# Squared-ReLU attention with a routed FFN: the last 64 keys move from the thirteenth to the eighth slot of a chunk

## The chip, the core and the metric

The kernel runs on one core of a Trainium2 chip. The metric is the time of one execution on the device in microseconds (us). Before the change it is 2067.73 us, the median of three runs (2067.33 to 2068.75). The five engines have queues of their own: PE multiplies matrices (its weight loads are listed as PEld), DVE, ACT and POOL work element by element, and SP issues the transfers.

## The reference, cut to what matters

```python
def _attn_ref(u, v, z):                      # u, v: 8 x 3136 x 256, z: 8 x 3136 x 64
    scale = 1.0 / S
    scores = scale * np.matmul(z, z.transpose(0, 2, 1))
    attn = np.maximum(scores, 0.0) ** 2
    return u * np.matmul(attn, v)

def _moe_ref(x, w_gate, w1, w2, capacity):   # capacity 128, F = 1024
    scores = np.einsum('bsd,d->bs', x, w_gate)
    out = x.copy()
    for b in range(B):
        top_idx = np.argpartition(-scores[b], capacity)[:capacity]
        xe = x[b, top_idx]
        ye = np.maximum(xe @ w1, 0.0) @ w2
        g = 1.0 / (1.0 + np.exp(-scores[b, top_idx]))
        out[b, top_idx] = x[b, top_idx] + g[:, None] * ye
    return out
```

For each of 8 batches, all 3136 keys weigh all 3136 queries by the square of a rectified product; the weighted sum of v is multiplied by u. Then the 128 tokens of the batch with the highest gate score go through a small FFN. All is float32.

## The kernel before

**Chunks and slots.** A batch is cut by queries into seven chunks: five of 512 columns (0 to 4), one of 256 and one of 320. For each chunk the 3136 keys are gone through in 13 *slots*: twelve with a pair of key tiles of 128 each, and one with the last 64 keys, which the code marks by `js == (NJ,)`. So there are 8 x 7 x 13 = 728 slots, in one list, `slots` (from line 319). Before the change the slot of 64 keys is the thirteenth of each chunk.

**What a slot does on PE.** float32 values are split into a high part `hi` and a low part `lo`, and v likewise. `mix` (line 523) adds a pair's share to the chunk's two accumulators, one for each half of the 256 columns of v: eight matmuls with `hi` and four with `lo`, all on line 556. The slot of 64 keys has four matmuls and no `lo` tile; its low half lies in the same tile as its high half. Its matmuls are also the last of the chunk: they carry `stop`, and `finish` (line 596) follows. In the first slot of a chunk (but the very first) the list is sorted by half, so a `lo` is read after four matmuls and not after eight. Three accumulator buffers serve all chunks: the second half of a new chunk needs the buffer that the first half of the old one frees.

**What it needs from the others.** A pair is *new* when its scores have to be made, or *old* when an earlier chunk has already made them (the score matrix is symmetric), stored them transposed, and they are fetched again. For a new pair, PE makes the scores with four matmuls (line 440) three slots ahead, in the middle of `mix`; ACT rectifies (line 450) and squares into `hi` (line 451); DVE squares once more in float32 (line 462), or ACT does (line 456); DVE or POOL subtracts to get `lo` (line 518); DVE transposes what later chunks want (lines 483 and 503), and SP stores it. For an old pair, ACT casts `hi` (line 418) and DVE or POOL makes `lo`. For the 64 keys, DVE does a square, a subtraction (line 474) and a transpose. An element-wise step goes to whichever of two engines a running tally, `busy`, says is less loaded.

**What sets the order.** The program is written out by hand, slot by slot, in the loop at the end (from line 1444). In slot k it issues first what `plan` holds for k: loads and preparations at fixed slot numbers, such as the next batch's z (`prep_z`, in the eighth slot of chunks 1 to 5, which puts a subtraction called ZL on POOL) and the chunk's u (`load_u`, in the eighth slot). Then comes `mix`, then the posts: the squares, `lo` parts and transposes of the pair three slots ahead, and with them DVE's share of a *near* task (multiplying a finished chunk by u, transposing it, the gate's sum) or a *far* task (choosing the tokens of the batch before, and its FFN). Far tasks run only in pair slots, and `rested` keeps them apart. Where the slot behind k is that of the 64 keys, the loop issues only the squares and holds the other posts back until that slot is over (lines 1502 to 1505):

```python
if k + 2 < len(slots) and len(slots[k + 1][2]) == 1:
    now = square_scores if c < WHOLE and (b or c) else settle_scores
    posts, held_posts = [now], [fn for fn in posts if fn is not settle_scores]
```

`finish` puts two instructions on DVE (line 601) that multiply the accumulators by u, and so free their buffers.

Of the kernel before, what the change touches and what calls it, by code (L numbers as in the profile page):

```python
# [88 lines left out]
def attention_then_routed_ffn(ctx: ExitStack, tc: tile.TileContext, zt, ut, v, wg, w1, w2, cst, cst16, keys, outs, at, cap):  # L89
    nc = tc.nc  # L90
    B, S, D = v.shape
# [14 lines left out]
    ROUNDS = 32 // BITS  # L106
    SHARES = P >> BITS
    SLOTS = NJ // 2 + 1

    const = ctx.enter_context(tc.tile_pool(name="const", bufs=1))  # L110
    vpool = ctx.enter_context(tc.tile_pool(name="vpool", bufs=NJ // 2))
# [204 lines left out]

    slots = []
    for b in range(B):  # L320
        for c in range(NCH):
            known = min(c, WHOLE) * GT + (2 if c > WHOLE and b < B - 1 else 0)
            old = [(2 * g, 2 * g + 1) for g in range(known // 2)]
            new = [(2 * g, 2 * g + 1) for g in range(known // 2, NJ // 2)]
            if c == WHOLE and b < B - 1:
                new.reverse()
            if c < WHOLE and (b or c):

                new.insert(len(new) - 2, new.pop(1))
            wait = 0.5 if (b, c) == (0, 1) else 0.0  # L330
            both = [(wait + (1 - wait) * (i + 0.5) / len(old), 0, js, True) for i, js in enumerate(old)]
            place = [(i + 0.5) / len(new) for i in range(len(new))]
            if b < B - 1 and c == NCH - 1:
                place = [1.6 / len(old)]
            both += [(x, 1, js, False) for x, js in zip(place, new)]
            slots += [(b, c, js, is_old) for _, _, js, is_old in sorted(both)]
            slots.append((b, c, (NJ,), False))
    assert len(slots) == B * NCH * SLOTS

    squares = [  # L340
# [185 lines left out]
    def mix(k, beside, between):  # L526


        b, c, js, _ = slots[k]
        assert k in parts  # L530
        hi, lo = parts.pop(k)
        first, last = k % SLOTS == 0, js[0] == NJ
        if first:
            acc[b, c] = [ps_a.tile([P, CH], F32, name="acc", tag="acc")[:, : CHUNKS[c][1]] for _ in range(NK)]
        ac = acc[b, c]
        todo = []
        if last:
            for h in range(NK):
                for w in range(2):
                    todo.append((h, V[b, NJ][:, w, h], hi[:, 0], w == 1))  # L540
        else:
            for h in range(NK):
                for q, j in enumerate(js):
                    for w in range(2):
                        todo.append((h, V[b, j][:, w, h], hi[:, q], False))
            for q, j in enumerate(js):
                for h in range(NK):
                    todo.append((h, V[b, j][:, 0, h], lo[:, q], False))
            if first and (b or c):
                todo.sort(key=lambda x: x[0])  # L550
        turn = (6 if c else 4) if first else 4 if last or len(slots[min(k + 1, len(slots) - 1)][2]) == 1 else 8
        done, lead, started = 0, 2, set()
        for n, (h, w, mov, stop) in enumerate(todo):
            if n == turn:
                between()
            nc.tensor.matmul(ac[h], w, mov, start=first and h not in started, stop=stop)  # L556
            started.add(h)
            upto = len(beside) * max(0, n - lead + 1) // (len(todo) - lead)
            for op in beside[done:upto]:
                op()  # L560
            done = max(done, upto)
        if turn == len(todo):
            if last:
                near.extend(finish(b, c))
            between()

    gate = {}
# [821 lines left out]
    def settle_stores():  # L1389
        for store in stores:  # L1390
            store()
        stores.clear()

    def took_by(k):
        _, c, js, is_old = slots[k]
        return CHUNKS[c][1] * 0.00045 * (6 if len(js) == 1 else 12 if is_old else 16)
# [53 lines left out]
    for k, (b, c, js, is_old) in enumerate(slots):  # L1450
# [8 lines left out]
        if len(js) == 2:  # L1459
            if near and (k % SLOTS or c <= NCH - late if late else k % SLOTS % 3 == 2):  # L1460
                tasks.append(near.popleft())
            if far and far[0] is None and not near and not tasks and not (late and c >= NCH - late):
                far.popleft()
                rested = k + 2
            if late and c >= NCH - late:

                left = sum(took_by(i) for i in range(k, k - k % SLOTS + SLOTS))
# [13 lines left out]
            elif (  # L1481
                far and far[0] and rested <= k and (busy["dve"] < 9 if late else not tasks)
                and (len(far[0]) < 4 or k % SLOTS != SLOTS - 3)
            ):
                task = far.popleft()
                rested = k + (task[2] if len(task) > 2 else 1 if late else 2)
                tasks.append(task[:2])
                if late and not near and rested == k + 1 and len(tasks) == 1 and far and not far[0][0] and busy["dve"] < 9:
                    tasks.append(far.popleft()[:2])
# [9 lines left out]
        now = settle_scores  # L1499
        posts = [*posts[:half], now, *posts[half:]]  # L1500
        held_posts = []
        if k + 2 < len(slots) and len(slots[k + 1][2]) == 1:

            now = square_scores if c < WHOLE and (b or c) else settle_scores
            posts, held_posts = [now], [fn for fn in posts if fn is not settle_scores]
# [9 lines left out]
        clock += took  # L1515
        if tasks:
            ready = max(told + 0.5, clock + 2.0)
        if len(js) == 1 and cap > 0:
            if c == NCH - 1 - late:
                far.extend([None, *route(b)])  # L1520
            elif c >= NCH - late:
# [64 lines left out]
```

## Time and profile before

| what | us |
|---|---|
| median of three runs | 2067.73 |
| the profiled execution | 2067.41 |
| its span | 2065.6 |
| PE busy in it | 2055.2 |
| DVE, POOL, ACT busy | 1529.0, 1357.5, 1291.2 |

The profiled execution lies 0.32 us under the median; 1.8 us of it lie around the span. A busy time is the union of an engine's instructions. Ends of matmuls are modelled, so two that follow each other closely overlap in the records, and a short wait may not show as idle time. Lines are those of the kernel before; in the changed kernel the same statements stand 1 to 6 lines lower in the part that matters here (556 becomes 562, 462 becomes 468, 601 becomes 607).

### The profile page before, as it was taken

The page shows a single profiled execution, that of the slowest core. Times are in us where ns is not written, and L with a number is a line of the kernel's source. Part 1 is how long each engine was busy: PE and PEld are TensorE (multiplying, and loading weights), DVE is VectorE, ACT ScalarE, POOL GpSimd, SP SyncE. Part 2 cuts the span into 40 slices and gives each one's busy share as a digit, 9 for nine tenths or more (in the row PEclk, how much of TensorE's full clock was granted, in tenths as well). Part 3 has the DMA queues.
Part 4 walks back from the last instruction along what each step waited for, and adds up shares of the span by engine and source line. Part 5 has one row for each costly group of instructions (what it writes and reads, how often), then busy time and mean ns, then how long its engine had stood idle before and what let it go on. Part 6 is the DMA issues. An engine that isn't in the chain of part 4 may idle for free.

```text
span 2065.6 us, 31660 instructions
## 1 busy us (share of the span) xinstructions
PE 2055.2 (99%) x10280; PEld 1744.5 (84%) x10280; DVE 1529.0 (74%) x2667; ACT 1291.2 (63%) x1629; POOL 1357.5 (66%) x728
## 2 busy tenths in 40 slices
PE   9999999999999999999999999999999999999999
PEld 6888988889888898888988889888898888888788
DVE  7676678856788667875678756887578876787776
ACT  7665576656775467664676546765477654775543
POOL 6766587756876468764677647875578755765643
PEclk9999999999999999999999999999999999999999
DMA  6788767886668765787767877678776776666862
GB/s 197 207 232 226 217 188 207 233 231 190 193 188 232 212 205 177 199 233 210 208 185 193 235 203 217 184 192 236 194 222 188 192 201 178 206 192 164 213 173 95
DMA packets 442758, 415.52 MB, mean 201 GB/s; under 512 B 133792, under 2 KB 374880, under 8 KB 439520
## 3 DMA queue, kind: packets, MB, share of 16 engines
q1 hardware_dynamic: 441456, 411.01, 70.9%
q0 software_dynamic: 768, 2.10, 0.3%
q8 instruction: 80, 1.31, 0.3%
q14 instruction: 86, 0.70, 0.1%
q10 hardware_dynamic: 368, 0.39, 0.1%
HBM read 238.78 MB, written 174.60 MB: 200 GB/s over the span
## 4 chain that ended last, share of the span: by engine, by line
PE 87%; DVE 3%; issue 2%; ACT 2%; DMA 2%; POOL 1%; SPq 1%; POOLq 0%; DVEq 0%; ACTq 0%
PE acc L556 73%; PE sc L440 12%; ACT hi L451 1%; POOL lo L518 1%; ACT a L450 1%; DVE a L462 1%; DVE aT L483 1%; PE h L1215 1%; PE y L1259 1%; DMA vst<-in_v 0%; DMA squares<-aT 0%; DVE lo L518 0%; DMA qk<-in_zt 0%; PE spread L680 0%; DMA qk<-squares_narrow 0%
## 5 line engine op out<-in xcount | busy, mean ns | idle before, releaser
L556 PE MATMUL acc<-hi,V 128*128 128x512 f32 (+2 forms) x5376 | 1218.4, 364 | 0.5
L518 POOL TENSOR_TENSOR lo<-a,hi 128x1024 fp32r<-128x1024 f32 (+2 forms) x326 | 717.9, 2204 | 563.5 <-DVE a L462 426.7
L556 PEld LDWEIGHTS acc<-hi,V 128*128 128x128 f32 x5376 | 932.9, 188 | 157.4 <-DVE ut L601 5.5
L556 PE MATMUL acc<-lo,V 128*128 128x512 f32 (+2 forms) x2688 | 664.0, 363 | 1.0 <-POOL lo L518 1.0
L450 ACT ACTIVATE a<-sc 128x1024 f32<-128x1024 f32 (+4 forms) x401 | 358.2, 893 | 449.2 <-PE sc L440 421.0
L556 PEld LDWEIGHTS acc<-lo,V 128*128 128x128 f32 x2688 | 471.1, 188 | 76.7 <-POOL lo L518 4.4
L462 DVE TENSOR_TENSOR a<-sc,a 128x1024 f32<-128x1024 f32 (+5 forms) x306 | 307.4, 1005 | 249.8 <-ACT hi L451 225.8
L418 ACT CAST hi<-qk 128x1024 fp32r<-128x1024 f32 (+2 forms) x327 | 279.7, 860 | 220.1 <-PE acc L556 198.1
L483 DVE STREAM_TRANSPOSE aT<-a 128x512 f32<-128x512 f32 (+3 forms) x541 | 349.5, 681 | 76.7 <-ACT a L456 54.4
L451 ACT ACTIVATE hi<-a 128x1024 fp32r<-128x1024 f32 (+4 forms) x401 | 372.2, 928 | 24.8 <-PE acc L556 2.3
L518 DVE TENSOR_TENSOR lo<-qk,hi 128x1024 fp32r<-128x1024 f32 (+2 forms) x220 | 319.2, 1459 | 81.7 <-ACT hi L418 79.3
L440 PE MATMUL sc<-Z,ZH 128*128 128x512 f32 (+2 forms) x746 | 275.1, 373 | 2.3 <-DVE a L462 2.1
L440 PE MATMUL sc<-Z,ZL 128*128 128x512 f32 (+2 forms) x746 | 273.3, 370 | 0.1
L518 POOL TENSOR_TENSOR lo<-qk,hi 128x1024 fp32r<-128x1024 f32 (+2 forms) x107 | 210.0, 1965 | 51.3 <-ACT hi L418 41.6
L440 PEld LDWEIGHTS sc<-Z,ZH 128*128 128x128 f32 x746 | 140.5, 188 | 31.7 <-DVE a L462 6.0
L440 PEld LDWEIGHTS sc<-Z,ZL 128*128 128x128 f32 x746 | 140.5, 188 | 24.7 <-DVE ZL L126 0.5
L126 POOL TENSOR_TENSOR V<-vst,V 128x512 fp32r<-128x512 f32 x92 | 136.5, 1489 | 29.8 <-ACT V L125 26.4
L622 POOL TENSOR_TENSOR ut<-x,w_run 128x1024 f32<-128x1024 f32 (+2 forms) x52 | 126.0, 2422 | 24.4 <-DVE x L613 23.4
L456 ACT ACTIVATE a<-a 128x1024 f32<-128x1024 f32 x93 | 98.8, 1062 | 2.9
L126 POOL TENSOR_TENSOR ZL<-zst,ZH 128x512 fp32r<-128x512 f32 (+2 forms) x56 | 84.2, 1508 | 2.5 <-ACT ZH L125 2.2
L125 ACT CAST V<-vst 128x512 fp32r<-128x512 f32 x95 | 57.9, 609 | 35.5 <-DMA vst<-in_v 35.5
L601 DVE SCALAR_TENSOR_TENSOR ut<-acc,ut 128x512 f32<-128x512 f32 (+2 forms) x112 | 63.9, 611 | 19.5 <-PE acc L556 19.2
(187 smaller groups left out, 1083.1 us busy)
## 6 DMA issues: line engine op xcount, KB each, us to landing
squares<-aT SPq DMA_DIRECT2D x160, 512.0 KB
qk<-squares SPq DMA_DIRECT2D x320, 256.0 KB
squares_narrow<-aT SPq DMA_DIRECT2D x320, 128.0 KB
qk<-squares_narrow SPq DMA_DIRECT2D x80, 512.0 KB
out<-x SPq DMA_DIRECT2D x162, 128.0 KB
ut<-in_ut SPq DMA_DIRECT2D x40, 512.0 KB
vst<-in_v SPq DMA_DIRECT2D x158, 128.0 KB
squares_own<-aT SPq DMA_DIRECT2D x39, 256.0 KB
```

The lines of the kernel that those rows point to most:

```text
L126: (lo_on or nc.vector.tensor_tensor)(lo, src, hi.bitcast(F32), op=ALU.subtract)
L418: nc.scalar.copy(by(hi), src)
L440: nc.tensor.matmul(ps[:, q], z[:, j * P : (j + 1) * P], mov, start=z is ZH, stop=z is ZL)
L450: nc.scalar.activation(a, ps[:, :n], AF.Relu)
L451: nc.scalar.activation(pieces[0][0](hi), pieces[0][1], AF.Square)
L456: nc.scalar.activation(a, a, AF.Square)
L462: square = lambda: nc.vector.tensor_tensor(a[rows], of[rows, :n], a[rows], op=ALU.mult)
L483: nc.vector.transpose(to, a[rows, q].rearrange("p (m t a) -> p m t a", m=GT, a=Q))
L518: on.tensor_tensor(view(lo), src, view(hi).bitcast(F32), op=ALU.subtract)
L556: nc.tensor.matmul(ac[h], w, mov, start=first and h not in started, stop=stop)
L601: nc.vector.scalar_tensor_tensor(xT[:, h, :w], acc[b, c][h], SCALE * SCALE, xT[:, h, :w], op0=ALU.mult, op1=ALU.mult)
L622: nc.gpsimd.tensor_tensor(wx, runs, consts["wg_run"].rearrange("p (o r) -> p o r", o=1).broadcast_to([P, NB, RUN]), op=ALU.mult,)
```

## The change

In chunks 1 to 4 of batches 0 to 6, the slot of 64 keys is put at index 7 of the chunk's 13 (`MIDDLE`), the eighth, and the pairs behind it move back by one. The chunk's last slot is then a pair: its last `lo` matmuls carry `stop`, its list is sorted by half like a first slot's, and `finish` follows it. The hold on posts ahead of the 64 keys does not apply in these chunks. `later` counts rests without the moved slot. All other chunks keep the old place.

```diff
--- before.py
+++ after.py
@@ -106,6 +106,7 @@
     ROUNDS = 32 // BITS
     SHARES = P >> BITS
     SLOTS = NJ // 2 + 1
+    MIDDLE = SLOTS // 2 + 1
 
     const = ctx.enter_context(tc.tile_pool(name="const", bufs=1))
     vpool = ctx.enter_context(tc.tile_pool(name="vpool", bufs=NJ // 2))
@@ -316,6 +317,10 @@
 
 
 
+    def inside(b, c):
+
+        return b < B - 1 and 0 < c < WHOLE
+
     slots = []
     for b in range(B):
         for c in range(NCH):
@@ -333,8 +338,9 @@
             if b < B - 1 and c == NCH - 1:
                 place = [1.6 / len(old)]
             both += [(x, 1, js, False) for x, js in zip(place, new)]
-            slots += [(b, c, js, is_old) for _, _, js, is_old in sorted(both)]
-            slots.append((b, c, (NJ,), False))
+            mine = [(b, c, js, is_old) for _, _, js, is_old in sorted(both)]
+            mine.insert(MIDDLE if inside(b, c) else len(mine), (b, c, (NJ,), False))
+            slots += mine
     assert len(slots) == B * NCH * SLOTS
 
     squares = [
@@ -529,15 +535,15 @@
         b, c, js, _ = slots[k]
         assert k in parts
         hi, lo = parts.pop(k)
-        first, last = k % SLOTS == 0, js[0] == NJ
+        first, last, rest = k % SLOTS == 0, k % SLOTS == SLOTS - 1, js[0] == NJ
         if first:
             acc[b, c] = [ps_a.tile([P, CH], F32, name="acc", tag="acc")[:, : CHUNKS[c][1]] for _ in range(NK)]
         ac = acc[b, c]
         todo = []
-        if last:
+        if rest:
             for h in range(NK):
                 for w in range(2):
-                    todo.append((h, V[b, NJ][:, w, h], hi[:, 0], w == 1))
+                    todo.append((h, V[b, NJ][:, w, h], hi[:, 0], last and w == 1))
         else:
             for h in range(NK):
                 for q, j in enumerate(js):
@@ -545,10 +551,10 @@
                         todo.append((h, V[b, j][:, w, h], hi[:, q], False))
             for q, j in enumerate(js):
                 for h in range(NK):
-                    todo.append((h, V[b, j][:, 0, h], lo[:, q], False))
-            if first and (b or c):
+                    todo.append((h, V[b, j][:, 0, h], lo[:, q], last and q == 1))
+            if first and (b or c) or last:
                 todo.sort(key=lambda x: x[0])
-        turn = (6 if c else 4) if first else 4 if last or len(slots[min(k + 1, len(slots) - 1)][2]) == 1 else 8
+        turn = (6 if c else 4) if first else 4 if rest or len(slots[min(k + 1, len(slots) - 1)][2]) == 1 else 8
         done, lead, started = 0, 2, set()
         for n, (h, w, mov, stop) in enumerate(todo):
             if n == turn:
@@ -559,9 +565,9 @@
             for op in beside[done:upto]:
                 op()
             done = max(done, upto)
+        if last:
+            near.extend(finish(b, c))
         if turn == len(todo):
-            if last:
-                near.extend(finish(b, c))
             between()
 
     gate = {}
@@ -1391,6 +1397,13 @@
             store()
         stores.clear()
 
+    def later(k, n):
+
+        while n:
+            k += 1
+            n -= not (k < len(slots) and len(slots[k][2]) == 1 and inside(*slots[k][:2]))
+        return k
+
     def took_by(k):
         _, c, js, is_old = slots[k]
         return CHUNKS[c][1] * 0.00045 * (6 if len(js) == 1 else 12 if is_old else 16)
@@ -1461,7 +1474,7 @@
                 tasks.append(near.popleft())
             if far and far[0] is None and not near and not tasks and not (late and c >= NCH - late):
                 far.popleft()
-                rested = k + 2
+                rested = later(k, 2)
             if late and c >= NCH - late:
 
                 left = sum(took_by(i) for i in range(k, k - k % SLOTS + SLOTS))
@@ -1483,7 +1496,7 @@
                 and (len(far[0]) < 4 or k % SLOTS != SLOTS - 3)
             ):
                 task = far.popleft()
-                rested = k + (task[2] if len(task) > 2 else 1 if late else 2)
+                rested = later(k, task[2] if len(task) > 2 else 1 if late else 2)
                 tasks.append(task[:2])
                 if late and not near and rested == k + 1 and len(tasks) == 1 and far and not far[0][0] and busy["dve"] < 9:
                     tasks.append(far.popleft()[:2])
@@ -1499,7 +1512,7 @@
         now = settle_scores
         posts = [*posts[:half], now, *posts[half:]]
         held_posts = []
-        if k + 2 < len(slots) and len(slots[k + 1][2]) == 1:
+        if k + 2 < len(slots) and len(slots[k + 1][2]) == 1 and not inside(b, c):
 
             now = square_scores if c < WHOLE and (b or c) else settle_scores
             posts, held_posts = [now], [fn for fn in posts if fn is not settle_scores]
@@ -1515,7 +1528,7 @@
         clock += took
         if tasks:
             ready = max(told + 0.5, clock + 2.0)
-        if len(js) == 1 and cap > 0:
+        if k % SLOTS == SLOTS - 1 and cap > 0:
             if c == NCH - 1 - late:
                 far.extend([None, *route(b)])
             elif c >= NCH - late:
```

How this moves instructions, at three places of batch 2. First PE, at the end of chunk 1 and the start of chunk 2 (`Vr` is the part of v of the 64 keys, `acc` the accumulators, `sc` scores of a later slot). Before:

```order
L556 MATMUL acc_5693<-lo_6035,V_5476 128x512
L556 MATMUL acc_5694<-lo_6035,V_5476 128x512
L556 MATMUL acc_5693<-hi_6049,Vr_5542 128x512 x2
L556 MATMUL acc_5694<-hi_6049,Vr_5542 128x512 x2
L440 MATMUL sc_6122<-Z_5910,ZH_96 128x512
L440 MATMUL sc_6122<-Z_5910,ZL_97 128x512
L440 MATMUL sc_6122<-Z_5910,ZH_96 128x512
L440 MATMUL sc_6122<-Z_5910,ZL_97 128x512
L556 MATMUL acc_6156<-hi_6085,V_5138 128x512 x4
L556 MATMUL acc_6156<-lo_6098,V_5138 128x512 x2
```

Now:

```order
L562 MATMUL acc_5693<-hi_6029,V_5476 128x512 x4
L562 MATMUL acc_5693<-lo_6052,V_5476 128x512 x2
L562 MATMUL acc_5694<-hi_6029,V_5476 128x512 x2
L446 MATMUL sc_6117<-Z_5918,ZH_96 128x512
L446 MATMUL sc_6117<-Z_5918,ZL_97 128x512
L446 MATMUL sc_6117<-Z_5918,ZH_96 128x512
L446 MATMUL sc_6117<-Z_5918,ZL_97 128x512
L562 MATMUL acc_5694<-hi_6029,V_5476 128x512 x2
L562 MATMUL acc_5694<-lo_6052,V_5476 128x512 x2
L562 MATMUL acc_6151<-hi_6068,V_5138 128x512 x4
L562 MATMUL acc_6151<-lo_6083,V_5138 128x512 x2
```

The four matmuls with `Vr` have left the end of the chunk. The twelve of its last pair stand there sorted by half, with the scores of a later slot between them.

Second DVE at the same place. `a` is a tile of rectified scores: 6011 of chunk 1's last pair, 6048 of the 64 keys and 6084 of chunk 2's first pair before; 6028 of chunk 1's last pair and 6067 of chunk 2's first pair now; `ge`, `own` and `least` belong to a routing step. Before:

```order
L462 TENSOR_TENSOR a_6011<-sc_6006,a_6011 128x1024
L483 STREAM_TRANSPOSE aT_6032<-a_6011 128x4x128 x2
L808 TENSOR_SCALAR ge_6060,own_6061<-gates_5631,least_6026 128x392
L814 STREAM_TRANSPOSE ge_6060<-own_6061 32x32 x4
L462 TENSOR_TENSOR a_6048<-sc_6045,a_6048 64x512
L474 TENSOR_TENSOR hi_6049<-a_6048,hi_6049 64x512
L483 STREAM_TRANSPOSE aT_6069<-a_6048 64x4x128
L462 TENSOR_TENSOR a_6084<-sc_6079,a_6084 128x1024
L503 STREAM_TRANSPOSE aT_6095<-a_6084 128x8x32 x2
L601 SCALAR_TENSOR_TENSOR ut_5952<-acc_5693,ut_5952 128x512
```

Now:

```order
L848 TENSOR_SCALAR least_6043<-k_sb_83,base_6041 32x1 x4
L468 TENSOR_TENSOR a_6028<-sc_6023,a_6028 128x1024
L489 STREAM_TRANSPOSE aT_6049<-a_6028 128x4x128 x2
L468 TENSOR_TENSOR a_6067<-sc_6062,a_6067 128x1024
L509 STREAM_TRANSPOSE aT_6080<-a_6067 128x8x32 x2
L814 TENSOR_SCALAR ge_6100,own_6101<-gates_5631,least_6043 128x392
L820 STREAM_TRANSPOSE ge_6100<-own_6101 32x32 x4
L607 SCALAR_TENSOR_TENSOR ut_5950<-acc_5693,ut_5950 128x512
```

The three instructions on 6048 are gone from between the square of chunk 1's last pair and that of chunk 2's first. A routing step stands in front of the accumulator's instruction.

Third POOL, in the middle of chunk 2 (6326, 6353, 6398 and 6461 are the `lo` parts of slots 7, 8, 9 and 11 before; 6292, 6394, 6419, 6445 and 6478 those of slots 6, 9, 10, 11 and 12 now; an index counts a chunk's slots from 0). Before:

```order
L518 TENSOR_TENSOR lo_6326<-qk_6151,hi_6307 128x1024
L518 TENSOR_TENSOR lo_6353<-a_6341,hi_6342 128x1024
L518 TENSOR_TENSOR lo_6398<-a_6377,hi_6378 128x8x64
L518 TENSOR_TENSOR lo_6398<-vst_6281,hi_6378 128x8x64
L126 TENSOR_TENSOR ZL_97<-zst_6222,ZH_96 128x4x4x32
L518 TENSOR_TENSOR lo_6461<-a_6449,hi_6450 128x1024
```

Now:

```order
L524 TENSOR_TENSOR lo_6292<-a_6268,hi_6269 128x1024
L524 TENSOR_TENSOR lo_6394<-a_6371,hi_6372 128x1024
L127 TENSOR_TENSOR ZL_97<-zst_6222,ZH_96 128x4x4x32
L524 TENSOR_TENSOR lo_6419<-a_6409,hi_6410 128x8x64
L524 TENSOR_TENSOR lo_6445<-qk_6188,hi_6430 128x1024
L524 TENSOR_TENSOR lo_6478<-a_6466,hi_6467 128x1024
```

ZL stood behind both instructions of the pair that is made in two pieces; now it stands in front of the first, and the second piece is DVE's.

## Rows read from the trace of the kernel before

**Rows 1.** Page, part 1: busy us, share of the span, instructions
```profile
span 2065.6 us, 31660 instructions
...
PE 2055.2 (99%) x10280; PEld 1744.5 (84%) x10280; DVE 1529.0 (74%) x2667; ACT 1291.2 (63%) x1629; POOL 1357.5 (66%) x728
```

**Rows 2.** Stretches of chunks 1 to 4: length, busy us per engine, clock, DMA
```profile
57.60:217.34 159.74, 159.65 (x718) 131.97 (x716) 108.63 (x124) 95.81 (x111) 107.94 (x52) 1.00 0.83 225
304.10:472.83 168.73, 167.76 (x770) 138.81 (x769) 127.66 (x249) 101.74 (x118) 108.18 (x54) 1.00 0.75 211
...
1323.39:1490.76 167.37, 167.37 (x770) 138.87 (x769) 126.46 (x248) 100.18 (x116) 106.69 (x52) 1.00 0.74 203
...
sum 1159.43, PE 1158.02 PEld 959.21 DVE 870.60 ACT 696.65 POOL 746.38; mean PE 165.43 PEld 137.03 DVE 124.37 ACT 99.52 POOL 106.62
```

**Rows 3.** Waits, engine PE: us in total, times, longest
```profile
PE sc L440 <- DVE a L462: 2.1, 4, 1.2
...
PE acc L556 <- POOL lo L518: 1.0, 2, 0.7
```

**Rows 4.** Stretches around chunk 2's first slot, batches 0, 1, 2, 5
```profile
97.88:103.43 5.55, 5.55 (x26) 4.55 (x25) 2.20 (x6) 3.87 (x5) 5.37 (x3) 1.00 0.38 144
345.45:351.97 6.52, 5.83 (x27) 4.48 (x26) 5.89 (x15) 4.71 (x6) 5.30 (x3) 1.00 0.60 161
600.40:606.53 6.13, 5.82 (x26) 4.48 (x25) 5.11 (x15) 4.44 (x5) 5.31 (x3) 1.00 0.65 164
...
1364.16:1369.89 5.73, 5.73 (x26) 4.48 (x25) 4.31 (x14) 4.04 (x5) 5.03 (x3) 1.00 0.67 169
...
sum 41.18, PE 40.17 PEld 31.43 DVE 30.49 ACT 29.26 POOL 36.20; mean PE 5.74 PEld 4.49 DVE 4.36 ACT 4.18 POOL 5.17
```

**Rows 5.** Timeline of PE, batch 2, start of chunk 2: start, us, instruction
```profile
602.30 1.07 PE L556 MATMUL acc<-hi,V 128*128 128x512 f32 x4
603.68 0.73 PE L556 MATMUL acc<-lo,V 128*128 128x512 f32 x2 [0.31 <-POOL lo L518]
...
606.53 1.98 PE L556 MATMUL acc<-hi,V 128*128 128x512 f32 x8
608.35 1.07 PE L556 MATMUL acc<-lo,V 128*128 128x512 f32 x4
```

**Rows 6.** Timeline of DVE, ACT and POOL just before that
```profile
597.84 0.69 DVE L462 TENSOR_TENSOR a<-sc,a 64x512 f32<-64x512 f32 x1
598.24 1.06 ACT L451 ACTIVATE hi<-a 128x1024 fp32r<-128x1024 f32 x1
598.57 0.69 DVE L474 TENSOR_TENSOR hi<-a,hi 64x512 fp32r<-64x512 f32 x1
599.18 0.70 DVE L483 STREAM_TRANSPOSE aT<-a 64x512 f32<-64x512 f32 x1
...
599.91 1.23 DVE L462 TENSOR_TENSOR a<-sc,a 128x1024 f32<-128x1024 f32 x1
...
601.22 2.41 POOL L518 TENSOR_TENSOR lo<-a,hi 128x1024 fp32r<-128x1024 f32 x1 [3.59 <-DVE a L462]
```

**Rows 7.** Timeline of PE, batch 2, chunk 2
```profile
616.51 1.98 PE L556 MATMUL acc<-hi,V 128*128 128x512 f32 x8
...
631.51 0.84 PE L556 MATMUL acc<-lo,V 128*128 128x512 f32 x3
```

**Rows 8.** Timeline of DVE and POOL, batch 2, chunk 2
```profile
626.85 1.18 DVE L631 TENSOR_REDUCE gate<-ut 128x16 f32<-128x1024 f32 x1
...
629.47 0.69 DVE L462 TENSOR_TENSOR a<-sc,a 128x512 f32<-128x512 f32 x1
...
631.55 1.29 POOL L518 TENSOR_TENSOR lo<-vst,hi 128x512 fp32r<-128x512 f32 x1
...
631.83 2.10 DVE L518 TENSOR_TENSOR lo<-qk,hi 128x1024 fp32r<-128x1024 f32 x1
...
632.80 2.28 POOL L126 TENSOR_TENSOR ZL<-zst,ZH 128x512 fp32r<-128x512 f32 x1
...
643.86 1.28 DVE L601 SCALAR_TENSOR_TENSOR ut<-acc,ut 128x512 f32<-128x512 f32 x2
```

## The prediction

> **What bounds the kernel now.** I read the page's table of engines first: PE is busy 2055.2 of the span's 2065.6 us, the other engines at most 74% [rows 1]. So the end is set by PE's queue, and what the change can give or cost is time in which PE stands. Second I cut out the stretches that the change touches: in each of batches 0 to 6, from the first matmul of chunk 1 to the second slot of chunk 5 (chunk 5's first slot still feels the end of chunk 4). PE is idle there for 1159.43 - 1158.02 = 1.41 us in all seven together, at a granted clock of 1.00 throughout [rows 2]. The batches repeat: batch 5 needs 167.37 us with no idle at all, batch 1 168.73. Third, the list of what PE waited for: little, and its waits for lo parts and for the squares of scores are the two kinds that the change can move [rows 3].
>
> The recorded idle time is not all of it, because the ends of matmuls are modelled and a short wait hides under the one before. I therefore compared lengths: the same 26 matmuls around the first slot of chunk 2 take 5.55 us in batch 0, 6.52 in batch 1, 6.13 in batch 2 and 5.73 in batch 5; the seven sum to 41.18 [rows 4]. Were all like batch 0, that would be 7 x 5.55 = 38.85. So 2.33 us go at this one place.
>
> Why there? In a chunk's first slot the matmuls are sorted by half of D, so a lo part is read after four matmuls, not after eight. In batch 2 the slot begins at 602.30, its lo matmuls only at 603.68, 0.31 us of it recorded as a wait for POOL [rows 5]. That lo (POOL, 601.22 to 603.63) waited for its square on DVE (599.91), and just in front of the square DVE did the three instructions of the last 64 keys: 597.84, 598.57, 599.18, together 0.69 + 0.69 + 0.70 = 2.08 us [rows 6]. ACT had the operand ready at 598.24 + 1.06 = 599.30. The short slot itself gives only four matmuls of cover: 8 matmuls go from 606.53 to 608.35, so 4 last 0.91 us [rows 5].
>
> **The change part by part.**
> *Matmuls.* None is added or removed: 12 in each pair slot, 4 for the 64 keys, as before. Cost 0; a reorder within a slot leaves the pace.
>
> *End of chunks 1 to 4.* The three DVE instructions no longer stand before the square for the next chunk's first pair, so it can begin at 599.30 instead of 599.91, 0.61 us earlier; and the slot before is now a pair of 12 matmuls, so the reader comes 8 matmuls = 1.82 us later. Together 2.4 us of new slack against a largest loss of 0.97 us (6.52 - 5.55). The waits at chunk 2's first slot go: minus 2.33 us. What is late next there is the release of the accumulator: the first of two DVE instructions of 1.28 us together (643.86 in batch 2 [rows 8]) must end before the second half of the next chunk's first slot. DVE now has the transposes of the next pair in front of it, at chunk 1's end a counting step too, but PE stands 4 + 4 matmuls further off, 1.82 us. I work that out for chunk 2's end below.
>
> *The last slot, now a pair sorted by half.* Its lo part is wanted after 4 matmuls instead of 8: 0.91 us sooner, or 1.82 where new scores stood between.
>
> *The middle.* The pairs that follow the short slot lose 1.82 us of lead. I walked chunk 2 of batch 2 by the new order with the durations of before. PE's slot 4 begins at 616.51 [rows 7]; with 0.227 us a matmul and the scores in their new places the readers of lo in slots 8, 9, 10 and 12 (counted from 0) come at 629.2, 632.9, 635.6 and 641.0 (before, the pair that is now in slot 9 was in slot 8 and read at 631.51 [rows 7]). DVE goes on at 616.8 as before, then has the keys' three instructions until 624.1 and a lo for slot 8 until 625.3: slack 3.9. The gate's reduce and a counting step (626.85 to 629.47 before, 2.6 us [rows 8]) end at 627.9; the square for slot 9 takes 1.23, POOL's lo 2.41: 631.6, slack 1.2. Then POOL has the batch's ZL, which now stands ahead of the lo for slot 10, where before it stood behind it. DVE's half of that lo runs until 632.3, ZL until 633.6, POOL's half until 634.9: slack 0.7, the tightest of the middle. The lo for slot 12 ends at 639.7: slack 1.3. The accumulator is released at 644.3, wanted at 645.1: slack 0.8. Chunks 1, 3 and 4, worked the same way, keep 1 us or more. So in the middle nothing is lost, if the walk holds to 0.7 us.
>
> One duration in it was a choice. DVE's lo at 631.83 took 2.10 us, and its end at 633.93 is 1.09 after POOL's lo (631.55 + 1.29 = 632.84); ZL, recorded from 632.80, took 2.28, ending 1.15 after DVE's [rows 8]. So each of the three in effect waited for the one before, and I added them up as 0.7, 1.29 and 1.29 in turn. The Trainium skill says the same in "SBUF — State Buffer", section "Who interferes with whom": a DVE instruction with two SBUF inputs and a GpSimd instruction that reads SBUF exclude each other for the whole instruction. Its point against this change is that whoever starts first keeps the other out, which makes the rival on ZL below. The trace agrees with the exclusion; in which order the two will start it can't show for the new program.
>
> *The rule on rests.* Routing and FFN steps keep two pair slots between them, so across the short slot one comes a slot later. Their work stays the same; a gate reduce with a counting step is 2.6 us of DVE, and one that falls before a square instead of behind it could cost, or return, what exceeds the slack there: bounds -0.6 (batch 1 is 1.36 us longer than batch 5, of which 6.52 - 5.73 = 0.79 lie in the first slot; the rest, 0.57, is a collision of this kind) to +2.6 us less 0.7 of slack, 1.9, in a batch or two. I take 0, nearest to batch 5, which shows none.
>
> *Loads.* The chunk's load of u and the preparation of the next z keep slot 7, now the short one; fetches keep seven slots of lead, one of them shorter by 1.82 us. Both are read several slots later; I put 0.
>
> **Sum.** -2.33 us. On the profiled execution's 2067.41 us that is 2065.1; the median of the timed runs is 0.32 above it, so 2065.4. As the runs of before spread by 1.4 us, this kernel's measurement tells about 0.2% (4.1 us) from no change; the forecast is inside that.
>
> **The rivals.**
> *Gain given back (0.25).* For it: slacks of 0.7 and 0.8 us in the walk are of the size of the waits that go, and new waits of 0.2 to 0.3 us in eight to ten chunks would eat 2.3 us. Against it: batch 5, which has all the old positions, shows no idle time, so most of the small slacks hold. Time 2067.7.
>
> *ZL goes first (0.08).* If POOL starts ZL before DVE's half of the lo for slot 10, that half waits for ZL's 1.29 us and ends at 633.6 + 0.7 = 634.3, still before POOL's own half; but what DVE does next, up to the square for slot 12, slips by 2.0 us, and that slot's lo from 639.7 to 641.7, 0.7 us behind its reader. In chunk 2 of up to 7 batches this costs 4.9 us: 2067.7 - 2.3 + 4.9 = 2070.3. For it: in the order, ZL is POOL's next instruction and its input is ready long before. Against: in the old order DVE's lo, waiting since 631.83, went ahead of a ZL in the same position [rows 8]. The skill's exclusion for whole instructions is what such a delay would follow from.
>
> *The middle becomes the wait (0.11), slower.* Place: the pairs in slots 8 to 10 and the last slot, in more than one chunk. Price: an event as in batch 2's chunk 2, 6.13 - 5.55 = 0.58 us; two chunks in each of seven batches make 14 x 0.58 = 8.1, less 2.3: 2073.5. It decides from the point where DVE or POOL comes over 0.7 us later than in my walk, in every batch alike, and is slower by more than 0.2% from 12 such events on. For it: POOL is fed by squares that stand behind counting steps. Against: ZL's 1.29 us are the only work that changes sides there.
>
> *More comes back (0.06).* The 2.33 us go, batch 1's 0.57 too, and the new rests take away waits outside the stretches: PE is idle for 10.4 us over the span [rows 1], 9.0 of them outside. 4.2 us in all would make 2063.5.
>
> Forecast 0.50. The range reaches down to 2063.4, with all but part of the last rival in, and up to 2071.6, through the one on ZL and to the edge of the slower one. Faster by over 0.2% is below 2063.6: 0.05. Slower by over 0.2% is above 2071.9: 0.11 and a little of the ZL rival, 0.12. The rest, 0.83, is no change.
>
> **What would show it.** In the trace after: the seven stretches at 167.4 us or under for batches 1 to 5, the 26 matmuls at the first slot of chunk 2 near 5.55 us, and no wait of PE for POOL's lo there: then the first step is right. A wait of PE for POOL's lo in slot 8, 9, 10 or 12, repeated in each batch, would show the middle wrong; PE's weight load waiting for DVE's accumulator step would show the release wrong. The prediction fails if PE's idle time in the seven stretches rises above 1.41 us.

## The result and the profile after

The changed kernel takes 2078.22 us (median of 6 runs, 2076.09 to 2080.78) against 2067.82 for the kernel before (6 runs, 2066.60 to 2068.75): a ratio of 1.0051, interval 1.0038 to 1.0064. It is 10.4 us slower, outside the range of the prediction, and on the side to which 0.12 was given.

The profiled execution is the longest of the six, 2080.78 us, 13.37 above that of before. Its trace therefore shows some 2.6 us more of the loss than the median has, and the cuts by chunk below are of this one execution.

The page, part 1, and the seven stretches of chunks 1 to 4 (the same as in [rows 2], found again by their matmuls; columns as there):

```profile
span 2079.0 us, 31659 instructions
...
PE 2059.9 (99%) x10280; PEld 1743.1 (84%) x10280; DVE 1601.0 (77%) x2702; ACT 1269.2 (61%) x1610; POOL 1331.7 (64%) x712
```

```profile
57.22:216.54 159.32, 159.32 (x717) 131.87 (x716) 120.62 (x131) 93.47 (x109) 103.14 (x47) 1.00 0.84 228
304.75:476.40 171.65, 168.73 (x771) 138.55 (x770) 137.17 (x253) 99.04 (x116) 103.31 (x51) 1.00 0.75 210
...
1334.04:1502.71 168.67, 167.75 (x771) 138.87 (x769) 136.75 (x253) 96.79 (x113) 101.22 (x49) 1.00 0.72 204
...
sum 1170.52, PE 1161.97 PEld 958.38 DVE 937.28 ACT 674.59 POOL 714.38; mean PE 166.00 PEld 136.91 DVE 133.90 ACT 96.37 POOL 102.05
```

The matmuls are as many as before and the clock is 1.00, but PE is idle for 1170.52 - 1161.97 = 8.55 us in the stretches, where it was 1.41 [rows 2]; they are 1170.52 - 1159.43 = 11.09 us longer. Batch 5, which had no idle time, now has 0.92. The other 2.3 us of the span's 13.4 lie outside them. The tally of loads has also given DVE 35 instructions more and POOL and ACT 16 and 19 fewer [rows 1].

Next the place where the gain was forecast, the first slot of chunk 2, in batches 0 and 1 and the sum [rows 4]:

```profile
97.24:102.77 5.53, 5.53 (x26) 4.56 (x25) 4.60 (x6) 3.66 (x5) 3.75 (x3) 1.00 0.37 142
345.53:351.06 5.53, 5.53 (x27) 4.55 (x25) 4.40 (x14) 3.17 (x4) 3.24 (x2) 1.00 0.18 59
...
sum 38.70, PE 38.70 PEld 31.90 DVE 31.02 ACT 22.69 POOL 23.18; mean PE 5.53 PEld 4.56 DVE 4.43 ACT 3.24 POOL 3.31
```

All seven take 5.53 us: 38.70 against 41.18, a gain of 2.48 us where 2.33 were predicted. So the loss is elsewhere, and larger than the net figure. The list of PE's waits, which answers to [rows 3], says where to look:

```profile
PE ahead L901 <- DVE upto L894: 4.6, 6, 1.2
PE acc L562 <- DVE lo L524: 2.0, 3, 1.3
PE sc L446 <- DVE a L468: 1.7, 3, 1.2
PE taken L942 <- DVE of L936: 1.5, 6, 0.3
```

Three of these are not in the list of before. The first and the last are not matmuls of attention. Both belong to the far task that chooses the tokens of the batch before: `ahead` is a matmul of 2 columns, `taken` one of 34. They come once in each of six batches. Cut by chunk (from a chunk's first matmul to the next one's), chunk 2 takes 289.49 us over batches 0 to 6 and chunks 3 and 4 together 569.57:

```profile
sum 289.49, PE 283.33 PEld 231.48 DVE 262.56 ACT 177.81 POOL 196.43; mean PE 40.48 PEld 33.07 DVE 37.51 ACT 25.40 POOL 28.06
sum 569.57, PE 567.18 PEld 467.18 DVE 406.43 ACT 282.75 POOL 273.84; mean PE 81.03 PEld 66.74 DVE 58.06 ACT 40.39 POOL 39.12
```

Before, the same cuts gave 284.04 and 563.23. So chunk 2 loses 5.4 us net of the gain at its start, and chunks 3 and 4 lose 6.3. The third new kind, the waits for DVE's `lo`, stands in chunk 3.

**Chunk 2.** The timeline of the changed kernel in batch 3 (start, us, engine, line, operation):

```profile
894.34 2.88 DVE L894 TENSOR_TENSOR_SCAN upto<-mk 98x32 bf16<-98x32 bf16 x2
894.75 2.39 POOL L524 TENSOR_TENSOR lo<-qk,hi 128x1024 fp32r<-128x1024 f32 x1
...
895.53 1.07 PE L562 MATMUL acc<-lo,V 128*128 128x512 f32 x4
...
897.14 1.19 DVE L468 TENSOR_TENSOR a<-sc,a 128x1024 f32<-128x1024 f32 x1
897.27 0.16 PE L901 MATMUL ahead<-upto,c 98*98 98x2 bf16 x1 [0.67 <-DVE upto L894]
```

and the same step in the kernel before, batch 2:

```profile
632.80 2.28 POOL L126 TENSOR_TENSOR ZL<-zst,ZH 128x512 fp32r<-128x512 f32 x1
...
634.06 1.22 DVE L888 TENSOR_TENSOR_SCAN upto<-mk 98x32 bf16<-98x32 bf16 x2
...
635.59 0.17 PE L895 MATMUL ahead<-upto,c 98*98 98x2 bf16 x1
```

Two scans over 98 x 32 numbers read both inputs from SBUF. After the change a subtraction of POOL's starts among them, at 894.75, runs its 2.39 us until 897.14, and the scans end only at 894.34 + 2.88 = 897.22. PE issues 0.05 us later: its queue is in order, so the four `lo` matmuls from 895.53 are the last that it can do until then. Before, the scans ended at 635.28, behind POOL's ZL (to 635.08), and PE asked for them at 635.59. They were held there too, but by the tail of a subtraction only, with 0.3 us to spare. The scans' durations over the whole program (count; shortest, median, longest in ns):

```profile
L894 DVE TENSOR_TENSOR_SCAN upto<-mk x14: 201/954/2423, 379.9 to 1877.1; 98x32 bf16<-98x32 bf16 x14
```

The `taken` step meets the same kind of hold a slot later: an addition on a 98 x 1 column (line 919, 913 before), held by the next `lo` on POOL, has a median of 1736 ns in the changed kernel,

```profile
L919 DVE TENSOR_TENSOR ahead<-quota,taken x7: 167/1736/1740, 387.2 to 1880.7; 98x1 f32<-98x1 f32 x7
```

and of 168 in the kernel before:

```profile
L913 DVE TENSOR_TENSOR ahead<-quota,taken x7: 167/168/169, 383.7 to 1867.4; 98x1 f32<-98x1 f32 x7
```

The Trainium skill has the rule for this in "SBUF — State Buffer", section "Who interferes with whom": a DVE instruction with two SBUF inputs contends with a GpSimd instruction that reads SBUF, the lock is exclusive, and issue order decides who blocks. The trace agrees, with 2.42 us for a scan that takes 0.20 at its shortest.

**Chunk 3.** Batch 1 of the changed kernel, SP's issues first, then DVE and PE:

```profile
397.84 0.62 SPq L199 DMA_DIRECT2D wh<-w1h_there  x1
398.51 0.68 SPq L199 DMA_DIRECT2D wl<-w1l_there  x1
...
404.71 0.56 SPq L495 DMA_DIRECT2D squares<-aT  x1
411.76 4.19 SPq L626 DMA_DIRECT2D out<-x  x4
...
417.11 1.31 DVE L489 STREAM_TRANSPOSE aT<-a 128x512 f32<-128x512 f32 x2 [4.73 <-DMA squares<-aT]
418.34 1.18 DVE L637 TENSOR_REDUCE gate<-ut 128x16 f32<-128x1024 f32 x1
419.44 1.21 DVE L524 TENSOR_TENSOR lo<-qk,hi 128x1024 fp32r<-128x1024 f32 x1
...
420.70 1.19 PE L562 MATMUL acc<-lo,V 128*128 128x512 f32 x4 [1.33 <-DVE lo L524]
```

Read it upwards. PE waits 1.33 us for a `lo` that DVE ended at 420.65. DVE had stood 4.73 us before a transpose, because the transposes have two buffers (`aT`) and the store that should free one had not landed. That store was issued at 404.71 and let DVE go at 417.11, 12.4 us later. The issues between 395 and 420, with KB each and median us from issue to landing, show the company it was in:

```profile
squares<-aT SPq DMA_DIRECT2D x2, 512.0 KB, 12.3
wh<-w1h_there SPq DMA_DIRECT2D x1, 1024.0 KB, 6.8
```

Over the whole run such a store lands in 3.3 us (median of 160). Here it follows the FFN's weights, of 1 MB each. DVE's waits for such stores sum to 27.0 us (before 16.0); one of 4.7 to 2.1 us stands at this place in each of batches 1 to 5.

### The profile page after: what moved, and what is told of

Read it like the earlier page. It is cut to its first block, busy times and chain, and to the rows that moved or that the text cites. A ratio compares the mean times of both kernels' runs of the same rounds, so it can differ in the third digit from the quotient of the medians.

```text
span 2079.0 us, 31659 instructions
## 1 busy us (share of the span) xinstructions
PE 2059.9 (99%) x10280; PEld 1743.1 (84%) x10280; DVE 1601.0 (77%) x2702; ACT 1269.2 (61%) x1610; POOL 1331.7 (64%) x712
## 4 chain that ended last, share of the span: by engine, by line
PE 76%; DVE 9%; DMA 6%; issue 3%; ACT 3%; SPq 2%; POOL 0%; POOLq 0%; DVEq 0%; ACTq 0%
PE acc L562 63%; PE sc L446 11%; DMA qk<-squares 3%; DVE a L468 2%; DVE aT L489 2%; DMA out<-x 1%; ACT a L456 1%; DVE lo L524 1%; ACT hi L457 1%; PE h L1221 1%; PE y L1265 1%; DMA qk<-squares_narrow 1%; DMA qk<-in_zt 1%; DMA vst<-in_v 1%; DVE ahead L919 1%
## 5 line engine op out<-in xcount | busy, mean ns | idle before, releaser
L524 POOL TENSOR_TENSOR lo<-a,hi 128x1024 fp32r<-128x1024 f32 (+2 forms) x317 | 706.6, 2232 | 575.8 <-DVE a L468 446.8
L468 DVE TENSOR_TENSOR a<-sc,a 128x1024 f32<-128x1024 f32 (+5 forms) x325 | 330.3, 1016 | 203.4 <-ACT hi L457 175.2
L524 DVE TENSOR_TENSOR lo<-qk,hi 128x1024 fp32r<-128x1024 f32 (+2 forms) x221 | 314.4, 1436 | 99.8 <-ACT hi L424 81.5
L462 ACT ACTIVATE a<-a 128x1024 f32<-128x1024 f32 x74 | 78.6, 1062 | 2.3
L127 POOL TENSOR_TENSOR ZL<-zst,ZH 128x512 fp32r<-128x512 f32 (+2 forms) x56 | 75.3, 1350 | 6.6 <-ACT ZH L126 6.6
```

The source lines that it names most:

```text
L127: (lo_on or nc.vector.tensor_tensor)(lo, src, hi.bitcast(F32), op=ALU.subtract)
L462: nc.scalar.activation(a, a, AF.Square)
L468: square = lambda: nc.vector.tensor_tensor(a[rows], of[rows, :n], a[rows], op=ALU.mult)
L524: on.tensor_tensor(view(lo), src, view(hi).bitcast(F32), op=ALU.subtract)
```

## The experiments

The theory was that there are two losses, each with one cause: the held scans in chunk 2, the late-freed buffer in chunk 3. The rivals: the slot in the middle costs in every chunk that has it; the scan edit saves time by itself, whatever the order; chunk 3 loses by its own order and not by what chunk 2 sends it.

Each kernel ran in five rounds beside the kernel before, with 5 executions (e2, e6) or 11 (the others); the changed kernel has its 6. The last two columns are the cuts by chunk of the profiled execution.

| kernel | median us | ratio to before, interval | chunk 2 | chunks 3 and 4 |
|---|---|---|---|---|
| before | | | 284.04 | 563.23 |
| after | 2078.22 | 1.0051, 1.0038 to 1.0064 | 289.49 | 569.57 |
| e1_outer | 2064.80 | 0.9989, 0.9980 to 0.9998 | 281.56 | 563.27 |
| e2_own_buffer | 2076.44 | 1.0043, 1.0029 to 1.0057 | 289.70 | 565.44 |
| e3_mask_psum | 2069.54 | 1.0012, 1.0003 to 1.0021 | 281.83 | 567.06 |
| e4_rest4 | 2069.32 | 1.0010, 1.0001 to 1.0019 | 281.88 | 566.96 |
| e5_not2 | 2065.45 | 0.9987, 0.9978 to 0.9996 | 281.56 | 562.89 |
| e6_not3 | 2075.58 | 1.0036, 1.0022 to 1.0050 | 289.44 | 565.16 |
| e7_before_psum | 2068.29 | 0.9999, 0.9990 to 1.0008 | | |
| e8_both | 2068.33 | 1.0001, 0.9992 to 1.0010 | 281.84 | 564.86 |

Medians of before were 2067.06 (e1 to e4), 2067.71 (e5 to e8) and 2067.82 (the changed kernel), so two kernels are best compared by how far each lies over the kernel before of its own rounds.

**Only chunks 1 and 4 take the new place.** The gain at chunk 2's start comes from the end of chunk 1, so this keeps it.

```diff
-        return b < B - 1 and 0 < c < WHOLE
+        return b < B - 1 and c in (1, 4)
```

> The 64 keys take the eighth slot in chunks 1 and 4 only, and the thirteenth in chunks 2 and 3 again. Theory A (the loss has two places of its own: the routing matmuls that PE holds in chunk 2, and the transposes in chunk 3 that wait for an earlier tile's store): both places get their old order back, and the wait at chunk 2's first slot stays away, so 2065.4 us (2064.5 to 2066.5), below the kernel before. Theory B (a short slot in the middle costs in any chunk, since DVE took over 19 squares and 15 half lo parts from ACT and POOL): half of the loss stays, 2072 to 2074. In the trace A wants the two stretches of chunks 2 and 3 without waits of PE, B wants new waits in chunks 1 and 4.

2064.80 us, 2.3 under before, as theory A had it. The first slots of chunk 2 sum to 38.70, as in the changed kernel, and the waits for scans and `lo` parts are gone from PE's list:

```profile
PE sc L446 <- DVE a L468: 1.7, 3, 1.2
PE idle L1420 <- DVE zero L1417: 1.2, 1, 1.2
PE xeT L1190 <- DMA xe<-out,ids: 0.4, 1, 0.4
```

So the slot in the middle costs nothing as such (two chunks have it here); what costs arises with chunks 2 and 3.

**The scans get one operand from PSUM.** The masks that they read lie in a PSUM bank, and the unused second operand is a constant.

```diff
-            mk = moe.tile([TP, 2 * NT], BF16, name="mk", tag="mk")[:R]
+            mk = st["ps"][:R, 128 : 128 + 2 * NT] if by_shares else moe.tile([TP, 2 * NT], BF16, name="mk", tag="mk")[:R]
...
-                nc.vector.tensor_tensor_scan(upto[:, part], st["mk"][:, part], st["mk"][:, part], 0.0, ALU.add, ALU.max)
+                if by_shares:
+                    most = consts["rank"][:R, :NT]
+                    nc.vector.tensor_tensor_scan(upto[:, part], st["mk"][:, part], most, 0.0, ALU.add, ALU.min)
```

> The change as it is, but the two scans of the routing step read one operand from PSUM and one from SBUF instead of two from SBUF (the running count is capped by its own rank, which changes nothing). Theory A, with exclusion between DVE and POOL: the second scan takes about 0.2 us instead of 2.42 beside POOL's lo part, so PE's six waits for it (4.6 us recorded) all but go: 2073.5 (2072.5 to 2075). The waits on the later matmul (taken), 0.41 us in each of six batches, stay or fall a little. Theory B, or no exclusion: the scans stay long, 2077 to 2079.

2069.54 us, 2.5 over the kernel before of its rounds, where the change is 10.4 over: 7.9 us saved, well over the 4.7 expected and outside the range given. Batch 3, the timeline:

```profile
888.36 0.34 DVE L896 TENSOR_TENSOR_SCAN upto<-tot,c_sb 98x32 bf16<-98x32 f32 x2
888.52 2.41 POOL L524 TENSOR_TENSOR lo<-qk,hi 128x1024 fp32r<-128x1024 f32 x1
...
890.24 0.17 PE L905 MATMUL ahead<-upto,c 98*98 98x2 bf16 x1
```

The same subtraction of 2.4 us runs beside the same scans, and they take 0.34 us together. Over the run (count; shortest, median, longest in ns):

```profile
L896 DVE TENSOR_TENSOR_SCAN upto<-tot,c_sb x12: 196/210/224, 378.7 to 1654.3; 98x32 bf16<-98x32 f32 x12
```

Chunk 2 falls from 289.49 to 281.83, 7.7 us, to within 0.3 of the kernel with only chunks 1 and 4 (281.56): the held scans account for chunk 2's loss. The list of waits put only 4.6 + 1.5 us on it. The waits for `taken` went with them, although its addition is held as in the changed kernel; the addition, and PE's wait for `taken`, in this kernel:

```profile
L923 DVE TENSOR_TENSOR ahead<-quota,taken x7: 169/1745/1754, 384.4 to 1869.5; 98x1 f32<-98x1 f32 x7
PE taken L946 <- DVE of L940: 0.3, 1, 0.3
```

So the hold on the addition costs PE little by itself; it showed in the changed kernel because the scan had already made DVE late.

**The step behind the scans rests two slots longer.** The scans stay as slow, PE's matmul comes later.

```diff
-            tasks.append(([], [lambda: settle_shares(last), lambda: (masks(), run_up())], 2, False))
+            tasks.append(([], [lambda: settle_shares(last), lambda: (masks(), run_up())], 4, False))
```

> The change as it is, but the rest behind the routing step with the scans is four pair slots instead of two, so PE meets the matmul that reads them in slot 12 of chunk 2 instead of slot 10, and all later steps of routing and FFN two slots later. Theory A: the 4.6 us of waits for the scans go; what follows falls on other slots, with 0 to 3 us of new waits: 2073 to 2076. Theory B: DVE is behind in any case, 2077 to 2080.

2069.32 us, 3.7 under the range that theory A gave; `ahead` moves to the last slot of chunk 2 and waits no more, and chunk 2 takes 281.88. Waits of PE for ACT's `hi` come in elsewhere, 4.8 us in all (0.8 in the changed kernel). The scans take as long as before the edit:

```profile
L894 DVE TENSOR_TENSOR_SCAN upto<-mk x14: 201/953/2451, 379.0 to 1868.0; 98x32 bf16<-98x32 bf16 x14
```

So, together with the scan edit, it is not DVE's lost time that counts but that PE stands in order behind a matmul of 2 columns.

**The scan edit in the kernel before.** A control; the masks lie in PSUM as above.

```diff
-                nc.vector.tensor_tensor_scan(upto[:, part], st["mk"][:, part], st["mk"][:, part], 0.0, ALU.add, ALU.max)
+                    nc.vector.tensor_tensor_scan(upto[:, part], st["mk"][:, part], most, 0.0, ALU.add, ALU.min)
```

> The kernel before, with the scans reading one operand from PSUM. Theory A: PE waited for no scan there, so there is nothing to gain: 2066.5 to 2068 (no change). Theory B (shorter routing steps help wherever they stand, as DVE is behind in any order): 2060 to 2064.

2068.29 us, ratio 0.9999: no change. The scans cost something only where PE is about to want them.

**A buffer of its own for the 64 keys' transpose**, in chunks 1 to 4.

```diff
+                if n == 1 and inside(b, c):
+                    t = moe.tile([P, GT, 1, P], F32, name="aTr", tag="hl", bufs=2)
+                else:
+                    t = work.tile([P, GT, 2, P], F32, name="aT", tag="aT", bufs=2)
```

> The change as it is, but the transposed scores of the 64 keys go to a buffer of their own in chunks 1 to 4, so that they no longer take one of the two that the pairs use in turn. Theory A: DVE's wait for the store (4.7 us in batch 1, chunk 3) goes, and with it PE's waits for the lo part of slot 9 there; these are 3.2 us over the batches (1.49 + 0.61 + 0.38 and smaller), so 2075 (2073.5 to 2076). Chunk 2's waits stay. Theory B: DVE's load is the same, 2077 to 2079.

2076.44 us, 1.4 above the value expected and a little outside the range given. Over the kernel before of its rounds that is 9.4, 1.0 less than the change's 10.4, and the two intervals overlap, so the times alone don't show a gain; the traces do. Chunks 3 and 4 fall from 569.57 to 565.44, and PE's waits for `lo` are gone; those of chunk 2 stay:

```profile
PE ahead L904 <- DVE upto L897: 4.8, 6, 1.2
PE sc L446 <- DVE a L468: 1.8, 3, 1.2
PE taken L945 <- DVE of L939: 1.6, 6, 0.3
PE acc L565 <- DVE ut L610: 1.3, 1, 1.3
```

The last line is a single event that the changed kernel has too, with 0.6 us. In batch 1 the stores at this place still land late, after 10.0 us in the median, but nothing waits for them. The buffer is the link by which chunk 3 loses. How much it loses by it is less sure, as the changed kernel's execution was its longest: with the scans cured the same buffer is worth 2.2 us there (567.06 to 564.86).

**All but chunk 2, and all but chunk 3.** Is chunk 3's loss its own, or does it come from what chunk 2 moves?

```diff
-        return b < B - 1 and 0 < c < WHOLE
+        return b < B - 1 and c in (1, 3, 4)
```

> The 64 keys in the eighth slot in chunks 1, 3 and 4, in chunk 2 in the thirteenth as before. Theory A, two places: chunk 2's waits (9.0 us after the change, 3.3 before) go, chunk 3's (6.7 after, 0.45 before) stay in part, 2068 to 2071. Theory C (chunk 3's waits are the echo of chunk 2's: the routing steps come late there, so weights and FFN steps fall together with the stores of chunk 3): 2064 to 2066, and no waits in chunk 3.

2065.45 us, where theory C had it: chunk 3 has the new order and loses nothing (chunks 3 and 4: 562.89). Chunk 3's waits need the move of chunk 2. The FFN's weights are issued here in batch 1 at

```profile
389.07 0.43 SPq L199 DMA_DIRECT2D wh<-w1h_there  x1
```

which is 3.05 us behind chunk 3's first matmul (386.02), as in the kernel before; in the changed kernel it is 8.05 (397.84 behind 389.79).

```diff
-        return b < B - 1 and 0 < c < WHOLE
+        return b < B - 1 and c in (1, 2, 4)
```

> The 64 keys in the eighth slot in chunks 1, 2 and 4, in chunk 3 in the thirteenth. Theory A: chunk 2's waits stay (6 waits for the scans and 6 for the choice, about 7 us), so 2071 to 2073. Theory C: much the same there, but chunk 3 also keeps waits in its old order, since the weights come late: 2073 to 2077.

2075.58 us, in theory C's range but not for its reason: chunk 2 keeps its loss (289.44), chunks 3 and 4 take 565.16, as with the buffer, and PE's list has no wait for a `lo`. Both moves together make chunk 3's loss: the move in chunk 2 puts the far steps behind it, the FFN's weights included, a slot later, and the move in chunk 3 puts the 64 keys' tile, which shares the two buffers, into the middle of that chunk. That the weights are what makes the store late is read from the trace; no run moved them alone. In this kernel, batch 1, the weights are issued as in the changed one (8.03 us behind 388.76), but SP goes straight on behind the store, where in the changed one it stood until 411.76, 6.4 us of it for the landing of `wl`:

```profile
396.79 0.63 SPq L199 DMA_DIRECT2D wh<-w1h_there  x1
397.46 0.69 SPq L199 DMA_DIRECT2D wl<-w1l_there  x1
...
403.19 0.56 SPq L495 DMA_DIRECT2D squares<-aT  x1
403.84 4.36 SPq L626 DMA_DIRECT2D out<-x  x4
```

**Both cures**: scans from PSUM and the buffer.

> The change with both edits: scans with one operand in PSUM, and an own buffer for the transposed scores of the 64 keys. Theory A: the two gains add, 8.7 and 1.8 us, so 2066 to 2068. Theory C: once the scans no longer hold PE up, the buffer matters little: 2069 to 2070.

2068.33 us, between the two ranges, with chunk 2 at 281.84, chunks 3 and 4 at 564.86 and the seven stretches 1.1 under before [rows 2]:

```profile
sum 1158.31, PE 1158.06 PEld 959.14 DVE 919.83 ACT 674.54 POOL 717.56; mean PE 165.44 PEld 137.02 DVE 131.40 ACT 96.36 POOL 102.51
```

The time only equals that of before (ratio 1.0001). DVE is still busy 49 us longer in the stretches than before, so its larger load is not what costs. Over the kernel before of its rounds this kernel lies by 0.6, the one with the scan edit alone by 2.5: the buffer gives 1.9 us on top of the scans, about the spread of the runs.

## Why the prediction was wrong

*What bounds the kernel:* right. PE's queue sets the end, and each loss was time in which PE stood.

*End of chunks 1 to 4, minus 2.33 us:* right. 2.48 us came at the place named. Kept without the rest, it is the best version: 2064.80 and 2065.45, both faster than before with their whole interval.

*The middle, nothing lost:* this step failed. Its slacks for `lo` were not what failed: in chunk 2 PE's list has no wait for a `lo`. The walk followed the readers of `lo` and the accumulator, with the durations of before. It left out the other readers in PE's queue, the matmuls of the far task, which stand there in order like the rest. And it gave DVE's small instructions no duration that depends on their neighbour, although the exclusion was used in the same walk for the large ones. The exclusion held a scan for 2.42 us, and cost 7.7 us in chunk 2. A row to read it from was there: the scans of before ended 0.31 us ahead of their reader, with one of the two already held by ZL.

*The release of the accumulator at chunk 2's end, slack 0.8:* this failed too, by less. With chunk 3 left out, some 2 us of chunks 3 and 4 stay (565.16 against 563.23), and they lie in chunk 3's first slot. From its first matmul to that of the next slot, summed over batches 1 to 6, in the kernel before and with chunk 3 left out, and a wait of PE's weight load there in batch 3 of the latter:

```profile
sum 21.84, PE 21.84 PEld 18.02 DVE 21.84 ACT 13.10 POOL 14.43; mean PE 3.64 PEld 3.00 DVE 3.64 ACT 2.18 POOL 2.40
sum 23.79, PE 23.79 PEld 18.07 DVE 17.90 ACT 9.63 POOL 16.70; mean PE 3.96 PEld 3.01 DVE 2.98 ACT 1.61 POOL 2.78
PEld acc L562 <- DVE ut L607: 0.4, 1, 0.4
```

Such a wait, of 0.3 to 0.4 us, stands in each of the six batches, in the changed kernel too, and in none of before: it is the sign that the prediction named for this. The `taken` step's instructions now stand on DVE just ahead (899.60 to 904.17 in batch 3 of the changed kernel). Of the 1.95 us some 0.6 are only the cut, since a small matmul of the far task now stands at chunk 3's start: with four slots of rest one stands there too, no weight load waits, and the sum is 22.42.

*The rule on rests, 0:* failed with these two, outside its bounds of -0.6 to 1.9. It counted what a step that falls a slot later does to a square on DVE. What mattered is that `ahead` came in slot 10 instead of 9 and its scans beside the `lo` of slot 11, and that the FFN's weights came a slot later.

*Loads, 0:* failed. The loads named there did no harm that the lists of waits show; the far task's weight loads were not counted among what moves. In chunk 3 they meet a store that frees one of two buffers: 4.1 us of the 6.3 go with the buffer (569.57 to 565.44), 4.4 with chunk 3's move (565.16).

*The rivals.* "The middle becomes the wait" had the sign, and its price of 2073.5 was the nearest, with 0.11. Its readers were the wrong ones, and what is said against it, that ZL's 1.29 us are the only work that changes sides, does not hold: the scans changed sides too. ZL's own place cost nothing visible. As events: six batches with one held scan, 7.7 / 6 = 1.3 us each, more than twice the 0.58 of that rival.

*Left open.* Outside the stretches the profiled executions lie between 0.7 us under before (chunks 1 and 4 alone) and about 4.7 over (chunk 3 left out), 2.3 over in the changed kernel, and 1.8 over with chunk 2 unmoved, so this is not tied to chunk 2. Among it are waits for ACT's `hi` in chunk 6, behind a load of v that lands late in one or two batches, with 3.0 us in two waits when chunk 3 is left out and 0.2 with chunks 1 and 4 alone. Why they differ from run to run was not tried. Nor was an order in which POOL's subtraction starts behind the scans.

## What to carry to other kernels

When work moves on an engine whose queue is in order, list every instruction in that queue as a reader, the matmul of 2 columns as well as the 12 of each slot, and give each the slack that the trace shows. Where a small DVE instruction reads both inputs from SBUF beside a POOL instruction that reads SBUF too, price it at the length of the POOL instruction that it may meet: 2.4 us here, not 0.2. It costs only where PE is about to want the result. When a step comes a slot later, follow its loads too, and ask which store they delay and which buffer that store frees.

## What the runs showed of the hardware

A scan of 98 x 32 took 0.20 us at its shortest, up to 2.42 with both operands in SBUF beside a subtraction on POOL, and 0.196 to 0.224 beside the same with one operand in PSUM; an addition on 98 x 1 numbers rose from 0.168 to 1.74. A store of 512 KB landed in 3.3 us in the median, and one issued behind two weight loads of 1 MB freed its buffer after 12.4. And the recorded waits of PE understated a loss: 6.1 us listed for the two steps in chunk 2, 7.7 recovered.
